# Position bias: two fp16 parts with a scale found on the chip in place of three bf16 parts, tables in blocks of 32 columns, one clamp on GpSimd

## The chip, the cores and the metric

One core of one Trainium2 chip. The metric is the device time of one execution, in microseconds; a profiled execution is read for the reasons. Engines in the rows: PE (TensorE matmuls), PEld (its weight loads), DVE (VectorE), ACT (ScalarE), POOL (GpSimd), SP (SyncE, which here only issues DMAs).

## The reference

Attention over 4 batches, 8 heads, 576 positions and 64 dimensions, all in fp32, with a bias on the scores that a small network makes from the positions, then a gated layer (2304 tokens, 512 wide, 1536 hidden):

```python
scores = scale * np.matmul(q, k.transpose(0, 1, 3, 2))
psi_rel = np.log1p(np.abs(rel)); psi_i = np.log1p(np.maximum(pos[:, None], 1.0))
x = (psi_rel / psi_i)[..., None]          # 576 x 576
h = np.maximum(x @ w1 + b1, 0.0)          # hidden 32
bias = h @ w2                             # 576 x 576 x 8 heads
attn = softmax(scores + bias); out = attn @ v
out = ((sigmoid(x @ w_gate) * (x @ w_val)) @ w_out)   # x: attention output, 2304 x 512
```

## The kernel before

Three stages follow each other: the position bias (to about 108 us of the span), attention (to about 370 us), the gated layer. Inside the stages the instructions of each engine stand in the order in which the program writes them; only matmuls, DMA landings and the other engines' progress set when each runs.

**The bias.** A hidden unit is active or not, depending on position; where it is active it adds `w1*w2*x + b1*w2`. So the bias of a query row i, column j and head h is `A*x + B`, where A and B are sums over the active units. The kernel makes the 0/1 switches first (tiles `ind` and `far`, 128 partitions = 4 columns times 32 units), and then adds up the coefficients by matmul: the switches are the stationary side (128 by 128), the coefficients `cfs` the moving side (64 columns: A and B, 8 heads, 4 groups). As a coefficient is fp32 and the matmul takes 16-bit input, `cf` (eight times the product of weights, line 311) is cut into three bf16 parts (lines 394 and 396), and `sums` (line 354) issues one matmul for each part with the same switches.

The stage runs over nine chunks of 64 columns (`c`, loop at 398). `switches(c)` gives a chunk's twelve `one` (two matmuls of 288 columns, line 332, and an eviction by ACT, line 337, or for four of chunk 0 by DVE, line 335) and three `apart` (comparisons on DVE, line 350); those of chunk c+1 are issued between the matmuls of chunk c at places listed in `YPOS` and `DPOS`. A chunk has five blocks of query rows, in the order `BORD` = 0, 1, 4, 2, 3. A block of 128 rows is 16 `sums`, block 4 (64 rows) is 8, so a chunk has 72 `sums`. After a block, `leave` (line 358) multiplies A by the table `xt` on DVE (line 364; 377 for block 4) and adds B (line 372): for blocks 1, 2, 3 on DVE straight from PSUM, in two instructions (heads 0 to 5, and 6 and 7), for block 0 (except in the last chunk) and block 4 after a copy by ACT (line 367) on POOL (lines 372, 382). The sums have two PSUM buffers of one block, the switches' matmuls two of their own.

**The order on the queues at the start.** SP issues small, lt(0), the tables xt, then lt(1). DVE runs `edges`, the weights `wy`, lines 303 to 305, and then what `own` holds: twelve switches in the order of `OWN` = 0 to 5 and 8 to 13; `CFI` says at which of them the five steps begin that cut `cf` (lines 394, 396), one at each switch. POOL makes `cf` (lines 308, 311) from the small load alone.

**Beside it,** `conv` (`narrow_ahead`, line 734) turns nine blocks of fp64 weights into fp32, one step after each block of rows: ACT takes the size (201), DVE clamps (204), shifts (207) and merges (210, 213), SP stores (750). `begun()` lets attention's first loads and preparation run in chunks 2, 6, 7 and 8.

**Attention** (line 542) reads the bias in the softmax's first instruction (line 567, 576 columns of one head and block of 128 rows); a unit is nine such steps, there are 16 units.

Of the kernel before, what the change touches and what calls it, by code (L numbers as in the profile page):

```python
# [39 lines left out]
CFI = 1  # L40
# [37 lines left out]
def host_layout(data):  # L78
# [12 lines left out]
        axis=1)), **data}  # L91
# [57 lines left out]
def tile_kernel(ctx, tc, q, k, v, small, w_gate, w_val, w_out, steps, lpos, xtab, lx, out, phases="0AB"):  # L149
# [8 lines left out]
    with ExitStack() as right, ExitStack() as att:  # L158
# [7 lines left out]
        biases = over.tile([128, 24, S], F32, name="bias0"), keep.tile([128, 8, S], F32, name="bias3")  # L166
# [11 lines left out]
        with tc.manual_schedule():  # L178
            bias(tc, small, steps, lpos, xtab, lx, biases, biasL, moe, lambda: next(attn))
        if "A" in phases:  # L180
            for _ in attn:
                pass
            att.close()
            if "B" in phases:
                moe.run()
        else:
            nc.sync.dma_start(out=out[0:512, 0:512].rearrange("(c p) j -> p c j", p=128), in_=biases[1][:, 4:8, 0:512])


def narrow(nc, t, lo, hi, eng, sized=None):  # L190
# [6 lines left out]
    def size():  # L197
        if sized:
            sized.tensor_scalar(out=t, in0=hi, scalar1=0x7FFFFFFF, scalar2=None, op0=ALU.bitwise_and)
        else:  # L200
            nc.scalar.activation(out=f, in_=hi.bitcast(F32), func=AF.Abs)
# [16 lines left out]
def bias(tc, small, steps, lpos, xtab, lx, biases, biasL, moe, begun):  # L218
# [6 lines left out]
    with ExitStack() as ph:  # L225
# [22 lines left out]
        lt = load_lx(0)  # L248
        dist = cp.tile([128, 2 * S], F16, name="dist")
# [10 lines left out]
        warm = ip.tile([128, 2, S], BF16, name="ind0")[:, 0, 0:512]  # L260
# [45 lines left out]
        cf = cp.tile([128, 2, H, 4], F32, name="cf")  # L306
        for ab in range(2):
# [3 lines left out]
            nc.gpsimd.tensor_scalar(out=cf[:, ab], in0=cf[:, ab], scalar1=wb[:, ab:ab + 1], scalar2=8.0, op0=ALU.mult, op1=ALU.mult)  # L311
        conv = moe.narrow_ahead(pool("cvw", 2), pool("cvm", 2))

        def switches(c, lt):

            np_, at = len(DPAIRS), S - 64 * c - 4 * DPAIRS[0]
            far = ip.tile([128, np_, 2 * S], BF16, name="far")
            pair = {i: far[:, n].rearrange("p (z s) -> p z s", z=2) for n, i in enumerate(DPAIRS)}
            pair.update({i: ip.tile([128, 2, S], BF16, name=f"ind{i}") for i in OWN if i < 8})
# [34 lines left out]
        def sums(o, st):  # L354
            for part in range(3):
                nc.tensor.matmul(out=o, lhsT=st, rhs=cfs[:, part], start=(part == 0), stop=(part == 2))  # L356

        def leave(ps, c, blk):
# [6 lines left out]
            if blk in BPOOL and c < NCH - 1 or blk == 4:  # L365
                rest, add = tp.tile([128, 2, H, 32], F32, name="brest")[:, 0:n], nc.gpsimd
                nc.scalar.activation(out=rest, in_=ps[:, 0:n, 1], func=AF.Copy)
            else:
                rest, add = ps[:, 0:n, 1], nc.vector
            if blk < 4:  # L370
                for t, h0, h1 in ((biases[0], 0, 6), (biases[1], 6, 8)):
                    add.tensor_tensor(  # L372
# [810 lines left out]
```

## Time and profile before

| | us |
|---|---|
| median of 3 runs (lowest, highest) | 803.34 (801.77, 805.56) |
| the profiled execution | 804.37 |
| its span | 802.60 |
| PE busy | 774.0 (96%) |
| DVE busy | 634.8 (79%) |
| ACT busy | 511.5 (64%) |
| POOL busy | 343.7 (43%) |

The span is what the profile covers, from the first to the last instruction; the execution's time has 1.8 us more around it. Busy time is the union of an engine's instructions, which overlap at their ends, so a mean length times a count is more than the busy time; a matmul's length holds its latency. Shares over the whole span say little about a stage, so the rows below are cut by stage.

### The profile page before, as it was taken

To read this page: it belongs to the slowest core of one execution; us is meant where nothing else is said; L and a number is where in the kernel's file an instruction comes from. 1 tells how busy PE (TensorE), PEld (TensorE's weight loads), DVE (VectorE), ACT (ScalarE), POOL (GpSimd) and SP (SyncE) were. 2 spreads that over 40 slices of the span, in tenths; PEclk is the share of its full clock that TensorE was granted. 3 is DMA by queue.
4 is the path that set the end of the run, shared out by engine and by line. 5 is a ranking of instruction groups with operands and counts; after the bars stand their busy time and mean duration, and the time that the engine had idled before them with its cause. 6 is when DMAs were issued, how large, how long until landed. Compare 5 with 4: busy or idle time off the path is not lost.

```text
span 802.6 us, 17329 instructions
## 1 busy us (share of the span) xinstructions
PE 774.0 (96%) x6356; PEld 722.8 (90%) x6356; DVE 634.8 (79%) x1301; ACT 511.5 (64%) x1094; POOL 343.7 (43%) x400
## 2 busy tenths in 40 slices
PE   7999989999999998899999999999999999999997
PEld 4888879999999998888998999889999999999996
DVE  6788888999999999896799899877877865656542
ACT  5888769989989987784444443554545546444442
POOL 1233559999989998951000000126233231523200
PEclk8999999999999999999999999999999999999999
DMA  5543434654664667747999633376334306321202
GB/s 198 152 147 126 130 97 125 176 167 131 180 172 127 180 178 205 212 125 234 367 313 297 203 132 131 118 220 220 111 106 145 105 27 212 129 73 64 75 1 79
DMA packets 66693, 124.21 MB, mean 155 GB/s; under 512 B 7344, under 2 KB 28976, under 8 KB 66608
## 3 DMA queue, kind: packets, MB, share of 16 engines
q1 hardware_dynamic: 64688, 120.15, 48.8%
q10 hardware_dynamic: 1920, 2.95, 1.2%
q8 instruction: 50, 0.82, 0.4%
q14 instruction: 35, 0.29, 0.1%
HBM read 86.04 MB, written 27.60 MB: 142 GB/s over the span
## 4 chain that ended last, share of the span: by engine, by line
PE 73%; DVE 13%; ACT 5%; DMA 4%; issue 3%; SPq 1%; POOL 0%; ACTq 0%; DVEq 0%
PE po L916 16%; PE pg L1018 12%; PE pu L1018 9%; PE sc L563 8%; PE acc L648 7%; PE pt L586 6%; PE pu L892 4%; PE pg L892 4%; PE bps L356 3%; DMA xin<-xs 2%; PE y L332 2%; DVE btmp L364 2%; ACT ind L337 1%; DVE en L567 1%; DVE bias L372 1%
## 5 line engine op out<-in xcount | busy, mean ns | idle before, releaser
L975 POOL TENSOR_TENSOR ws<-wm 128x256 f32<-128x256 f32 x44 | 41.4, 940 | 301.6 <-DMA wm<-scratch 147.0
L570 ACT ACTIVATE en<-en,mn 128x576 f32<-128x576 f32 x144 | 111.5, 774 | 31.7 <-DVE mn L567 30.7
L1018 PE MATMUL pg<-xq,wv 128*128 128x384 f32 x576 | 117.2, 338 | 1.0 <-ACT c L1044 1.0
L563 PE MATMUL sc<-k,QS 128*128 128x288 f32 x640 | 112.2, 301 | 1.4 <-DVE bias L372 0.6
L1018 PEld LDWEIGHTS pg<-xq,wv 128*128 128x128 f32 x576 | 103.2, 188 | 9.7 <-ACT c L1044 1.7
L567 DVE CUSTOM_DVE_ANT_0 en<-sc,bias 128x576 f32<-128x576 f32 x128 | 93.9, 751 | 7.4 <-PE sc L563 6.4
L1024 DVE TENSOR_TENSOR c<-pu,c 128x384 f32<-128x384 f32 x72 | 40.1, 557 | 74.5 <-PE pu L1018 29.3
L563 PEld LDWEIGHTS sc<-k,QS 128*128 128x128 f32 x640 | 92.0, 189 | 2.8 <-PE sc L563 0.8
L586 PE MATMUL pt<-ident,en 128*128 128x128 f32 x576 | 87.5, 275 | 3.1 <-DVE aL L486 1.9
L916 PE MATMUL po<-wo,gh 128*128 128x512 f32 x288 | 89.6, 392 | 0.0
L1018 PE MATMUL pu<-xq,wv 128*128 128x384 f32 x432 | 87.6, 337 | 0.4 <-DVE g L902 0.3
L1018 PEld LDWEIGHTS pu<-xq,wv 128*128 128x128 f32 x432 | 76.6, 188 | 3.3 <-DVE g L902 0.8
L648 PE MATMUL acc<-aH,vv 128*128 128x288 f32 x240 | 76.3, 334 | 3.2 <-DVE xe L651 3.0
L586 PEld LDWEIGHTS pt<-ident,en 128*128 128x128 f32 x576 | 68.7, 141 | 6.6 <-ACT en L570 3.4
L486 DVE TENSOR_TENSOR aL<-pt,aH 128x512 fp32r<-128x512 f32 (+1 forms) x112 | 66.6, 607 | 7.1 <-ACT aH L485 7.1
L356 PE MATMUL bps<-cfs,ind 128*128 128x64 bf16 x1458 | 67.4, 193 | 3.1 <-DVE bias L372 2.4
L337 ACT ACTIVATE ind<-y 128x576 bf16<-128x576 f32 x100 | 62.1, 653 | 10.5 <-PE y L332 8.2
L356 PEld LDWEIGHTS <-ind 128*128 128x128 bf16 x1458 | 58.6, 98 | 9.6 <-DVE bias L372 4.2
L648 PE MATMUL acc<-aL,vv 128*128 128x288 f32 x240 | 67.1, 296 | 0.0
L1036 ACT ACTIVATE gh<-c 128x384 fp32r<-128x384 f32 x48 | 25.2, 526 | 62.9 <-DVE c L1034 62.9
L490 POOL TENSOR_TENSOR aL<-ar,aH 128x512 fp32r<-128x512 f32 x48 | 62.4, 1300 | 4.0
L1044 ACT ACTIVATE c<-pg 128x384 f32<-128x384 f32 x72 | 35.1, 487 | 38.0 <-PE pg L1018 37.1
(152 smaller groups left out, 1913.4 us busy)
## 6 DMA issues: line engine op xcount, KB each, us to landing
wm<-scratch SPq DMA_DIRECT2D x48, 256.0 KB, 2.6
wo<-parts SPq DMA_DIRECT2D x24, 512.0 KB, 5.2
kr<-in_k_dram SPq DMA_DIRECT2D x32, 288.0 KB
QS<-part SPq DMA_DIRECT2D x64, 144.0 KB, 2.5
xs<-xe SPq DMA_DIRECT2D x32, 288.0 KB, 3.5
xin<-xs SPq DMA_DIRECT2D x48, 192.0 KB, 4.0
parts<-w SPq DMA_DIRECT2D x12, 512.0 KB, 10.0
vr<-in_v_dram SPq DMA_DIRECT2D x16, 320.0 KB, 3.6
```

The lines of the kernel that those rows point to most:

```text
L337: nc.scalar.activation(out=o, in_=y[:, :, 0:HF], func=AF.Sigmoid, scale=float(2.0 ** 64))
L356: nc.tensor.matmul(out=o, lhsT=st, rhs=cfs[:, part], start=(part == 0), stop=(part == 2))
L486: return lambda: nc.vector.tensor_tensor(out=lo, in0=ps, in1=hi.bitcast(F32), op=ALU.subtract)
L490: nc.gpsimd.tensor_tensor(out=lo, in0=src, in1=hi.bitcast(F32), op=ALU.subtract)
L563: nc.tensor.matmul(out=ps[:, e, 0:HF], lhsT=l, rhs=r[:, HF * e:HF * e + HF], start=(i == 0), stop=(i == len(mms) - 1))
L567: nc.vector.tensor_tensor_reduce(out=half(en), in0=ps[:, :, 0:HF], in1=half(nbias), scale=-0.125, scalar=3.0e38, op0=ALU.add, op1=ALU.min, ...
L570: nc.scalar.activation(out=en, in_=en, func=AF.Exp, bias=mn, scale=-1.0, accum_out=sm)
L586: nc.tensor.transpose(pt[:, J], en[:, 128 * J:128 * J + 128], ident)
L648: nc.tensor.matmul(out=acc[:, 0:HF], lhsT=l, rhs=r, start=(i == 0), stop=(i == len(mms) - 1))
L892: self.nc.tensor.matmul(out=(pg, pu)[z], lhsT=l, rhs=r, start=(kc == 0 and i == 0), stop=(kc == 3 and i == 2))
L916: self.nc.tensor.matmul(out=po, lhsT=l[:, tt], rhs=r, start=(first and i == 0), stop=(last and i == 2))
L1018: nc.tensor.matmul(out=p, lhsT=W[i][:, l, at + kc], rhs=V[b][:, r, kc], start=(new and n == 0), stop=(n == 5), skip_group_check=not new)
```

## The change

Coefficients: `cf` is scaled by `up`, a power of two, and cut into two fp16 parts; the switches are fp16 tiles. The scale comes from the largest absolute product of weights, found on the chip: a new input `wide` (w2 repeated over 128 partitions, 128 KB) is loaded by SP after lt(0), POOL multiplies it with w1 and b1 (2 x 8 x 32 values and a floor of 2^-100), DVE reduces to the largest and takes its exponent bits, POOL scales `up` and the inverse `un`. The tables xt are multiplied by `un` on POOL, and B is multiplied by `un` where it is evicted: as the scale of ACT's copy, or by a scalar_tensor_tensor in place of DVE's tensor_tensor. `CFI` goes from 1 to 8, so the now three steps stand at the ninth to eleventh switch. The bias tables become blocks of 32 columns, [18, 4, heads, 32], written block by block and read by the softmax through a pattern of 32-column runs. `narrow_ahead` passes GpSimd as the engine of the clamp.

```diff
@@ -37,7 +37,7 @@
 WARM = 12
-CFI = 1
+CFI = 8
@@ -88,7 +88,7 @@
         [np.repeat(w1, 128, 0), np.repeat(b1, 128, 0), picks(), np.tile(w1.T, (4, 1)), np.tile(b1.T, (4, 1)), np.tile(w2, (4, 1))],
-        axis=1)), **data}
+        axis=1)), "wide": np.repeat(w2.T.reshape(1, H * HID), 128, 0), **data}
@@ -163,7 +163,7 @@
         make_identity(nc, ident)
-        biases = over.tile([128, 24, S], F32, name="bias0"), keep.tile([128, 8, S], F32, name="bias3")
+        biases = over.tile([128, 18, 4, 6, 32], F32, name="bias0"), keep.tile([128, 18, 4, 2, 32], F32, name="bias3")
@@ -246,6 +243,8 @@
         lt = load_lx(0)
+        wd = cp.tile([128, H, HID], F32, name="wide")
+        nc.sync.dma_start(out=wd.rearrange("p h m -> p (h m)"), in_=wide)
@@ -257,7 +256,7 @@
             nc.sync.dma_start(out=xt[64 * e:64 * e + 64, 4, 0:S - 32 * e], in_=xtab[512:576, 32 * e:S])
-        warm = ip.tile([128, 2, S], BF16, name="ind0")[:, 0, 0:512]
+        warm = ip.tile([128, 2, S], F16, name="ind0")[:, 0, 0:512]
@@ -304,19 +303,35 @@
         cf = cp.tile([128, 2, H, 4], F32, name="cf")
+        fit = cp.tile([128, 3], F32, name="fit")
+        big, up, un = (fit[:, i:i + 1] for i in range(3))
+        both = cp.tile([128, 2 * H * HID + 1], F32, name="both")
+        nc.gpsimd.memset(both[:, 2 * H * HID:], 2.0 ** -100)
+        nc.gpsimd.tensor_tensor(
+            out=both[:, 0:2 * H * HID].rearrange("p (z h m) -> p z h m", z=2, h=H),
+            in0=wd.rearrange("p (o h) m -> p o h m", o=1).to_broadcast([128, 2, H, HID]),
+            in1=wr.rearrange("p z (o m) -> p z o m", o=1).to_broadcast([128, 2, H, HID]), op=ALU.mult)
+        nc.vector.tensor_reduce(out=big, in_=both, axis=mybir.AxisListType.X, op=ALU.max, apply_absolute_value=True)
+        nc.vector.tensor_scalar(out=up.bitcast(I32), in0=big.bitcast(I32), scalar1=0x7F800000, scalar2=0x7F800000, op0=ALU.bitwise_and, op1=ALU.bitwise_xor)
+        nc.vector.tensor_scalar(out=un.bitcast(I32), in0=big.bitcast(I32), scalar1=0x7F800000, scalar2=None, op0=ALU.bitwise_and)
+        for o, z in ((up, 13), (un, -11)):
+            nc.gpsimd.tensor_scalar(out=o, in0=o, scalar1=float(2.0 ** z), scalar2=None, op0=ALU.mult)
...
                 in1=group.rearrange("p (o g) -> p o g", o=1).to_broadcast([128, H, 4]), op=ALU.mult)
-            nc.gpsimd.tensor_scalar(out=cf[:, ab], in0=cf[:, ab], scalar1=wb[:, ab:ab + 1], scalar2=8.0, op0=ALU.mult, op1=ALU.mult)
+            nc.gpsimd.tensor_scalar(out=cf[:, ab], in0=cf[:, ab], scalar1=wb[:, ab:ab + 1], scalar2=up, op0=ALU.mult, op1=ALU.mult)
+        for blk in BORD:
+            x = xt[:, blk, 0:S if blk < 4 else S - 32]
+            nc.gpsimd.tensor_scalar(out=x, in0=x, scalar1=un, scalar2=None, op0=ALU.mult)
...
             np_, at = len(DPAIRS), S - 64 * c - 4 * DPAIRS[0]
-            far = ip.tile([128, np_, 2 * S], BF16, name="far")
+            far = ip.tile([128, np_, 2 * S], F16, name="far")
             pair = {i: far[:, n].rearrange("p (z s) -> p z s", z=2) for n, i in enumerate(DPAIRS)}
-            pair.update({i: ip.tile([128, 2, S], BF16, name=f"ind{i}") for i in OWN if i < 8})
+            pair.update({i: ip.tile([128, 2, S], F16, name=f"ind{i}") for i in OWN if i < 8})
@@ -352,8 +367,8 @@
         def sums(o, st):
-            for part in range(3):
-                nc.tensor.matmul(out=o, lhsT=st, rhs=cfs[:, part], start=(part == 0), stop=(part == 2))
+            for part in range(2):
+                nc.tensor.matmul(out=o, lhsT=st, rhs=cfs[:, part], start=(part == 0), stop=(part == 1))
@@ -364,14 +379,17 @@
                 rest, add = tp.tile([128, 2, H, 32], F32, name="brest")[:, 0:n], nc.gpsimd
-                nc.scalar.activation(out=rest, in_=ps[:, 0:n, 1], func=AF.Copy)
+                nc.scalar.activation(out=rest, in_=ps[:, 0:n, 1], func=AF.Copy, scale=un)
...
                 for t, h0, h1 in ((biases[0], 0, 6), (biases[1], 6, 8)):
-                    add.tensor_tensor(
-                        out=t[:, blk::4, js].rearrange("p h (s j) -> p s h j", s=2),
-                        in0=rest[:, :, h0:h1], in1=tmp[:, :, h0:h1], op=ALU.add)
+                    o, a, b = t[:, 2 * c:2 * c + 2, blk], rest[:, :, h0:h1], tmp[:, :, h0:h1]
+                    if add is nc.gpsimd:
+                        add.tensor_tensor(out=o, in0=a, in1=b, op=ALU.add)
+                    else:
+                        o, a, b = (z.rearrange("p s h j -> p s (h j)") for z in (o, a, b))
+                        add.scalar_tensor_tensor(out=o, in0=a, scalar=un, in1=b, op0=ALU.mult, op1=ALU.add)
@@ -383,16 +401,16 @@
         ind, own, far = switches(0, lt)
-        cfs = cp.tile([128, 3, 2, H, 4], BF16, name="cfs")
+        cfs = cp.tile([128, 2, 2, H, 4], F16, name="cfs")
...
             part, sub = divmod(i - CFI, 2)
-            if part in range(3):
+            if part in range(2):
...
                     nc.vector.tensor_copy(out=cfs[:, part], in_=cf)
-                elif part < 2:
+                elif part < 1:
@@ -551,12 +569,12 @@
             h, it = divmod(s, 4)
-            nbias = biases[0][:, 8 * p + s] if p < 3 else biases[1][:, s]
+            nbias = biases[0][:, :, it, 2 * p + h] if p < 3 else biases[1][:, :, it, h]
...
         else:
-            nbias = biasL[:, p]
+            nbias = biasL[:, p].rearrange("p (j m) -> p j m", m=32)
@@ -565,7 +583,8 @@
             nc.vector.tensor_tensor_reduce(
-                out=half(en), in0=ps[:, :, 0:HF], in1=half(nbias), scale=-0.125, scalar=3.0e38,
+                out=en.rearrange("p (e j m) -> p e j m", e=2, m=32), in0=ps[:, :, 0:HF].rearrange("p e (j m) -> p e j m", m=32),
+                in1=nbias.rearrange("p (e j) m -> p e j m", e=2), scale=-0.125, scalar=3.0e38,
@@ -746,7 +765,7 @@
                 going.append([
-                    lambda: None, lambda: None, *narrow(nc, m, w[:, :, :, 0], w[:, :, :, 1], nc.vector),
+                    lambda: None, lambda: None, *narrow(nc, m, w[:, :, :, 0], w[:, :, :, 1], nc.gpsimd),
...
```

## Rows read from the trace of the kernel before

**Rows 1.** Windows: length; busy of PE, PEld, DVE, ACT, POOL; clock; DMA share; GB/s

```profile
16.67:27.79 11.12, 10.23 (x250) 9.27 (x247) 7.36 (x15) 9.49 (x16) 3.21 (x6) 1.00 0.36 114
27.79:90.05 62.26, 59.12 (x1459) 53.26 (x1456) 53.28 (x115) 53.49 (x94) 23.27 (x40) 1.00 0.48 149
90.05:100.27 10.22, 9.32 (x243) 8.32 (x239) 8.85 (x20) 7.16 (x13) 6.48 (x10) 1.00 0.47 137
100.27:108.35 8.08, 5.62 (x159) 5.06 (x155) 7.21 (x17) 1.67 (x2) 3.14 (x5) 1.00 0.40 118
124.20:139.40 15.20, 15.20 (x124) 14.99 (x123) 13.86 (x37) 13.79 (x34) 14.28 (x16) 1.00 0.56 146
```

**Rows 2.** Timeline of PE, chunk 0: start us, length us, instruction, count

```profile
15.07 0.69 PE L356 MATMUL bps<-cfs,ind 128*128 128x64 bf16 x18 [0.31 <-ACT ind L337]
...
15.77 0.69 PE L356 MATMUL bps<-cfs,ind 128*128 128x64 bf16 x18
```

**Rows 3.** Groups by line and shape, 27.79 to 90.05: busy us, mean ns, idle

```profile
L356 PE MATMUL bps<-cfs,ind 128*128 128x64 bf16 x990 | 46.7, 193 | 0.6 <-DVE bias L372 0.2 <-ACT brest L367 0.2
...
L356 PE MATMUL bps<-cfs,far 128*128 128x64 bf16 x324 | 18.3, 193 | 0.0
L364 DVE TENSOR_TENSOR btmp<-bps,xt 128x512 f32<-128x512 f32 x25 | 17.2, 689 | 4.5 <-PE bps L356 4.2
```

**Rows 4.** Timeline of ACT, chunk 3

```profile
53.05 1.79 ACT L337 ACTIVATE ind<-y 128x576 bf16<-128x576 f32 x3
```

**Rows 5.** Timeline of DVE, chunks 3 and 4; brackets: idle before, releaser

```profile
54.63 0.69 DVE L364 TENSOR_TENSOR btmp<-bps,xt 128x512 f32<-128x512 f32 x1 [0.92 <-PE bps L356]
...
56.03 0.42 DVE L204 TENSOR_SCALAR cvm<-cvm 128x512 f32<-128x512 f32 x1
...
57.99 0.42 DVE L207 TENSOR_SCALAR cvm<-cvm 128x512 int32<-128x512 int32 x1
```

**Rows 6.** Timeline of DVE, the start

```profile
6.89 0.35 DVE L295 SCALAR_TENSOR_TENSOR btmp<-wh,small,btmp 128x128 f32<-128x128 bf16 x1
7.16 0.29 DVE L297 TENSOR_TENSOR btmp<-btmp,wh 128x128 f32<-128x128 f32 x1
...
10.15 0.19 DVE L394 CAST cfs<-cf 128x64 bf16<-128x64 f32 x1
...
14.79 0.76 DVE L335 TENSOR_SCALAR ind<-bps 128x576 bf16<-128x576 f32 x1
```

**Rows 7.** Timeline of POOL, the start

```profile
3.94 0.25 POOL L308 TENSOR_TENSOR cf<-small 128x32 f32<-128x32 f32 x1 [2.18 <-DMA small<-in_small_dram]
...
5.04 0.52 POOL L311 TENSOR_SCALAR cf<-cf,small 128x32 f32<-128x32 f32 x1
```

**Rows 8.** Groups by line and shape, 0 to 200 us

```profile
L479 POOL TENSOR_SCALAR aH<-ar 128x512 fp32r<-128x512 f32 x18 | 11.1, 619 | 4.2 <-PE sc L563 2.1 <-ACT ar L599 1.9
...
L499 ACT ACTIVATE part<-qr 128x576 fp32r<-128x576 f32 x8 | 5.5, 684 | 0.0
...
L281 ACT ACTIVATE pos<-pos,et 128x576 f32<-128x576 f32 x1 | 0.8, 774 | 1.7 <-DVE et L278 1.7
```

**Rows 9.** Timeline of POOL, chunks 7 and 8

```profile
99.40 0.66 POOL L479 TENSOR_SCALAR k<-kr 128x576 fp32r<-128x576 f32 x1
```

**Rows 10.** Timeline of DVE, chunks 7 and 8

```profile
99.56 0.78 DVE L207 TENSOR_SCALAR cvm<-cvm 128x512 int32<-128x512 int32 x1
...
105.39 0.69 DVE L364 TENSOR_TENSOR btmp<-bps,xt 128x512 f32<-128x512 f32 x1 [0.73 <-PE bps L356]
```

**Rows 11.** The page's costliest groups of instructions, whole span

```profile
L567 DVE CUSTOM_DVE_ANT_0 en<-sc,bias 128x576 f32<-128x576 f32 x128 | 93.9, 751 | 7.4 <-PE sc L563 6.4
...
L563 PEld LDWEIGHTS sc<-k,QS 128*128 128x128 f32 x640 | 92.0, 189 | 2.8 <-PE sc L563 0.8
...
L356 PEld LDWEIGHTS <-ind 128*128 128x128 bf16 x1458 | 58.6, 98 | 9.6 <-DVE bias L372 4.2
...
L490 POOL TENSOR_TENSOR aL<-ar,aH 128x512 fp32r<-128x512 f32 x48 | 62.4, 1300 | 4.0
```

More of the change, by code (lines that the diff above doesn't have):

```diff
@@ L148, in tile_kernel @@
 @with_exitstack
-def tile_kernel(ctx, tc, q, k, v, small, w_gate, w_val, w_out, steps, lpos, xtab, lx, out, phases="0AB"):
+def tile_kernel(ctx, tc, q, k, v, small, wide, w_gate, w_val, w_out, steps, lpos, xtab, lx, out, phases="0AB"):
     nc = tc.nc
@@ L178, in tile_kernel @@
         with tc.manual_schedule():
-            bias(tc, small, steps, lpos, xtab, lx, biases, biasL, moe, lambda: next(attn))
+            bias(tc, small, wide, steps, lpos, xtab, lx, biases, biasL, moe, lambda: next(attn))
         if "A" in phases:
@@ L186, in tile_kernel, with narrow @@
         else:
-            nc.sync.dma_start(out=out[0:512, 0:512].rearrange("(c p) j -> p c j", p=128), in_=biases[1][:, 4:8, 0:512])
-def narrow(nc, t, lo, hi, eng, sized=None):
+            nc.sync.dma_start(out=out[0:512, 0:512].rearrange("(c p) j -> p c j", p=128), in_=biases[1][:, 0:16].rearrange("p a b h j -> p a (b h j)").rearrange("p (c z) m -> p c (z m)", c=4)[:, :, 0:512])
+def narrow(nc, t, lo, hi, eng):
     f = t.bitcast(F32)
     def size():
[L198 to L201, printed above, removed]
+        nc.scalar.activation(out=f, in_=hi.bitcast(F32), func=AF.Abs)
     def clamp():
@@ L215, in narrow, with bias @@
     return size, clamp, low, top, tail
-def bias(tc, small, steps, lpos, xtab, lx, biases, biasL, moe, begun):
+def bias(tc, small, wide, steps, lpos, xtab, lx, biases, biasL, moe, begun):
     nc = tc.nc
```

## The prediction

> **What bounds the kernel now.** I read the table of windows first, cut where the first table multiply of a chunk starts (line 364). The position bias is built in nine chunks before attention. In the six whole chunks from 27.79 to 90.05 us PE is busy 59.12 of 62.26 us, ACT 53.49, DVE 53.28 and POOL 23.27 [rows 1]. So a chunk takes 62.26/6 = 10.38 us, in which PE works 9.85 (95%), ACT 8.92, DVE 8.88: PE is the bound, but two other engines stand 0.9 us below it. After this stage PE is busy 15.20 of 15.20 us in a unit of attention [rows 1], so what the stage gives back moves the rest forward as a block, and the change touches nothing behind it but the layout that the softmax reads.
>
> The timeline gives PE's price: 18+6 small matmuls take from 15.07 to 15.77, 0.70/24 = 29.2 ns each, although a row calls one 193 ns long (they are pipelined) [rows 2, 3]. A chunk has 72 products with three matmuls, 216 x 29.2 = 6.31 us of PE; the rest of its 9.85, 3.54 us, are mostly the 24 wide matmuls of line 332. (The 990+324 rows in six chunks are 219 a chunk, the cut being in the middle of a block [rows 3].) DVE's timeline shows the same bound: at 54.63 it had been idle 0.92 us for PE [rows 5]. ACT's evictions of line 337 go back to back at about 0.60 us (three in 1.79) [rows 4].
>
> **The change, part by part.** **Two parts for three.** 72 matmuls fewer a chunk: 72 x 29.2 = 2.10 us, PE's work falls to 7.75. No row shows a matmul in fp16. The nearest are these bf16 ones, same shape, same bytes: 29.2 ns. The other end is the fp32 kind, whose weight loads are named 189 ns against 98 here [rows 11], about twice, so 58 ns. I take the nearer row. The Trainium skill, "TensorE: Matmul & The Clock Gate", section "Weight-path perf modes", says the fast weight load is on for 128 weights of any type that isn't FP32; by it fp16 costs what bf16 does, and no run here shows it yet. The 0/1 tables are now written as fp16, two bytes as before: nothing.
>
> **What is late next.** PE at 7.75 no longer holds the chunk; ACT (8.92) and DVE (8.88) do, and their own changes decide.
>
> ACT: its two evictions a chunk at line 367 get a scale read per partition. The nearest rows: an Exp with such a scale over 576 elements 774 ns, a plain Copy of the same shape 684 [rows 8]; so 0 to 0.09 us each, 0 to 0.18 a chunk. I take half: ACT 9.0.
>
> DVE: the clamp (line 204, 0.42 us [rows 5]) goes to POOL, nine of them in some seven chunks: -0.5 us a chunk. Against that six adds of a chunk (line 372) become scalar_tensor_tensor with a per-partition scalar. Such an instruction over 128 elements took 0.35 us, a plain tensor_tensor of that size right behind it 0.29 [rows 6]: +0.06 each, +0.36 a chunk, or 0 if the length alone counts. DVE 8.4 to 8.75. The output in runs of 32 columns costs nothing I can see: line 364 already reads in runs of 32 and takes 689 ns for 512 elements, the softmax without them 751 for 576, 1.35 and 1.30 ns an element with the fixed part in it [rows 3, 11].
>
> POOL has room (23.27 of 62.26 busy [rows 1]) for nine clamps of about 0.62 us (its copy of 512 elements: 619 ns [rows 8]). But the clamp now queues behind POOL's adds of the same block, and DVE's next conversion step (line 207) waits for it, with DVE's next table work queued behind. Where the block is 0 or 4, POOL starts those adds late, so two or three of the nine can cost DVE 0.3 to 0.6 us, hidden in part. I take 0.3 us in all. A row speaks against the change: line 207 took 0.78 us instead of 0.42 at 99.56 while POOL ran a copy from 99.40 to 100.06 [rows 5, 9, 10]: the two engines get in each other's way. The Trainium skill, "SBUF - State Buffer", section "Who interferes with whom", has the rule: one port pair is shared, locked for a whole instruction, and the other engine stands still; the row agrees (0.36 us lost). By it a clamp of 0.62 us on POOL could take from DVE more than the 0.42 it gives; that is the first rival.
>
> So ACT at 9.0 is the longest, DVE close behind. PE now fills 95% of a chunk as the bound; with two near-equal engines I take the same share, 9.0/0.95 = 9.45 us. Ends: 8.92 (ACT alone, no stall) and 10.0 (first rival).
>
> **The start.** The new 128 KB load goes into SP's queue ahead of the table loads and delays them by little; nobody waits for those before 16.7. POOL then makes 512 products (1.30 us as its other 128x512 [rows 11]), early, if the load is there. On DVE the reduction stands where the first cast of line 394 stood (10.15 [rows 6]): about 0.69 as line 364 [rows 3], two one-column operations of 0.1, so the queue is 0.9 later at 11.1. POOL then scales twice and makes the coefficients, four operations that took from 3.94 to 5.56 before [rows 7]; with the two scalings about 2.3 us, done near 13.4. DVE reaches the first cast (CFI 8) only around 14.1, and saves two of the five small operations of 0.2. The last cast is at about 15.3, the last switch (14.79 before [rows 6]) starts at about 15.3 too, and PE starts its products near 15.4 instead of 15.07, with a third fewer of them ahead of the first add. Net 0.2 us late; ends: 0.3 early, and 3 late if the load only lands when the first loads are all through. POOL's scaling of the tables (5 x 0.67 us [rows 9]) comes just behind, the first block done before it is used.
>
> **The last chunk** has DVE busy 7.21 of 8.08 us [rows 1]; its idle is one wait of 0.73 for PE [rows 10], of which PE gives back most, while eight scalar adds cost 0.5. Zero, within 0.6 either way.
>
> **The sum.** Chunks 1 to 7 (62.26 + 10.22 us [rows 1]): 7 x (10.35 - 9.45) = 6.3. Chunk 0, 11.12 us with ACT at 9.49 [rows 1], goes to 9.49/0.95 = 10.0: 1.1. Less 0.2 for the start and 0.3 for the clamps: 6.9 us. The profiled execution took 804.37 us (span 802.60), so 797.5. The median of the runs is 1.0 below it, so 796.4 from there; I forecast 796.8. Perfect overlap gives 7 x (10.35 - 8.92) + 11.12 - 9.49 = 11.6, from the median 791.7. Chunks of 10.0 us give 7 x 0.35 = 2.5, with 0.6 of chunk 0, less 0.3 and a start 0.9 late: 1.9, or 802.5 from the profiled time and 801.4 from the median; a start 3 us late takes all of that.
>
> **The rivals.** **DVE takes the place of PE.** The scalar costs 0.36 a chunk, and clamps and adds collide on the shared way into memory: 0.62 x 1.25 clamps = 0.78 a chunk. DVE then needs 8.75 + 0.78 = 9.5, /0.95 = 10.0 us: gain 2 to 3 us, about 801.5. For it: the 0.78 us row. Against: POOL is idle six tenths of the stage, line 207 met POOL in one row and took 0.42 elsewhere. Chance 0.20.
>
> **Slower: the softmax pays for the blocks.** Line 567 now reads its table in 18 pieces of 32 columns, far apart, and writes in the same shape. A unit of attention has nine of them and DVE is busy 13.86 of 15.20 us [rows 1]: 1.34 spare, 149 ns each. If each grew by x, PE would lose (9x - 1.34) us in each of 16 units; the 6.9 us of gain are gone at x = 0.198, a softmax of 0.95 us against 0.75 now. At 1.0 us: 0.9 x 16 = 14.4, less 6.9: about 811. Against it: line 364's price per element above. Chance 0.05.
>
> **Slower: fp16 runs slower on PE.** With p ns a matmul PE needs 144p + 3.54; at p = 44 it is back at 9.85 us and the start is lost; at 58 ns a chunk is 11.9/0.95 = 12.5, eight chunks give 17 us, about 821. Nothing in the trace speaks for it. Chance 0.03. That the change doesn't do what it says can be read directly: 144 matmuls a chunk.
>
> PE's clock is no rival: the granted clock is 1.00 in all of these windows (the 2.4 GHz level), also in the last chunk with PE busy 5.62 of 8.08 [rows 1], a lower share than I expect in any chunk but the last.
>
> **How the numbers follow.** Forecast (pitch 8.9 to 9.8) 0.72, DVE bound 0.20, slower 0.08. The range 791.5 to 802.0 takes in the first two. Half a per cent, 4 us, is about what a measurement of this kernel can tell from no change: below 799.3 counts as faster, 0.72; the DVE case is the same, 0.20; slower 0.08.
>
> **What would show it.** In the trace after: bps matmuls at about 29 ns, 1296 in all; chunks of 9.2 to 9.7 us with PE near 80%, ACT and DVE above 90%, the waits now PE's for ACT (line 337) and DVE (line 372); line 372 at 0.06 us more or nothing; clamps of 0.62 on POOL; first add of a table within 1 us of 16.67; softmax at 0.75. I am wrong if chunks stay at 10 us with DVE full, if PE's first product slips past 17 us, or if attention's units leave 15.2 us.

## The result, and the profile after

The median went from 803.43 us (801.77 to 805.56, 4 runs) to 809.66 us (809.01 to 810.12, 4 runs): ratio 1.008, 95% interval 1.0056 to 1.0104. The kernel is 6.4 us slower (the ratio times 803.4); the forecast was 6.5 us faster. The profiled execution took 809.34 us, its span is 807.6, 5.0 more than before.

The windows of after, cut as in [rows 1] (columns as there), and one microsecond of its last chunk:

```profile
17.39:28.38 10.99, 9.12 (x184) 7.81 (x181) 8.74 (x16) 9.37 (x17) 8.66 (x10) 1.00 0.36 129
28.38:94.22 65.84, 49.77 (x1011) 41.33 (x1008) 53.50 (x106) 54.14 (x94) 37.58 (x48) 1.00 0.44 137
94.22:103.92 9.70, 7.42 (x169) 6.21 (x166) 8.82 (x18) 6.84 (x12) 7.72 (x9) 1.00 0.40 120
103.92:111.89 7.97, 4.48 (x103) 4.15 (x98) 7.27 (x14) 1.76 (x2) 6.31 (x8) 0.79 0.38 109
108.00:109.00 1.00, 0.85 (x17) 0.86 (x18) 1.00 (x2) 0.11 (x1) 0.59 (x1) 0.50 0.00 0
```

PE has less to do, as promised: 49.77 us in six chunks in place of 59.12 (8.30 a chunk; the prediction had 7.75). Yet the six chunks take 65.84 us in place of 62.26: 10.97 each. No engine is full: DVE 81%, ACT 82%. POOL went from 23.27 to 37.58 us. The 5.0 us of span are 0.72 at the start (first add at 17.39, not 16.67), 2.93 in chunks 0 to 7 (86.53 against 83.60), 1.15 from there to the first matmul of the scores (7.97 against 6.82; in before that matmul starts at 107.09, inside the last window of the stage), and 0.2 in all the rest.

The groups by line and shape of after, 0 to 112 us, that hold the change (us busy, mean ns, idle before):

```profile
L201 POOL TENSOR_SCALAR cvm<-cvm 128x512 f32<-128x512 f32 x9 | 17.9, 1992 | 0.5
L392 DVE SCALAR_TENSOR_TENSOR bias<-bps,fit,btmp 128x384 f32<-128x384 f32 x27 | 16.7, 618 | 1.0
...
L392 DVE SCALAR_TENSOR_TENSOR bias<-bps,fit,btmp 128x128 f32<-128x128 f32 x27 | 9.2, 341 | 0.0
...
L326 POOL TENSOR_SCALAR xt<-xt,fit 128x576 f32<-128x576 f32 x4 | 6.9, 1733 | 0.0
```

In before, 0 to 200 us:

```profile
L372 DVE TENSOR_TENSOR bias<-bps,btmp 128x384 f32<-128x384 f32 x28 | 15.6, 558 | 1.0
...
L372 DVE TENSOR_TENSOR bias<-bps,btmp 128x128 f32<-128x128 f32 x28 | 7.9, 281 | 0.0
...
L210 DVE SCALAR_TENSOR_TENSOR cvm<-cvw,cvm 128x512 int32<-128x512 int32 x9 | 6.1, 682 | 0.0
```

And from the page's costliest groups, over the whole span:

```profile
L585 DVE CUSTOM_DVE_ANT_1 en<-sc,bias 128x576 f32<-128x576 f32 x128 | 93.8, 752 | 7.3 <-PE sc L581 6.3
...
L371 PE MATMUL bps<-cfs,ind 128*128 128x64 f16 x972 | 52.8, 195 | 17.7 <-DVE bias L392 10.9
```

The clamp on POOL (line 201) takes 1.99 us, not 0.62; the scaling of a table (line 326) 1.73, not 0.67. The adds with a scalar take 618 and 341 ns; without it they took 558 and 281 in before. The softmax (line 585) is where it was [rows 11], and the products (line 371) wait 10.9 us for DVE.

The list of waits of after, 17 to 113 us (us in all, times, longest):

```profile
ACT brest L382 <- DVE btmp L379: 10.9, 8, 2.9
PE bps L371 <- DVE bias L392: 10.9, 18, 1.9
...
DVE cvm L204 <- POOL cvm L201: 6.2, 4, 2.2
```

DVE stands still 6.2 us for the clamp, with the table work of the next block queued behind that wait; and PE stands still behind DVE's adds.

Last chunk of after, timelines of DVE, POOL and PE:

```profile
105.43 1.14 DVE L207 SCALAR_TENSOR_TENSOR cvm<-cvw,cvm 128x512 int32<-128x512 int32 x1
106.50 0.68 DVE L379 TENSOR_TENSOR btmp<-bps,xt 128x512 f32<-128x512 f32 x1
...
108.00 1.14 DVE L210 SCALAR_TENSOR_TENSOR cvm<-cvw,cvm 128x512 int32<-128x512 int32 x1
```

```profile
104.62 1.41 POOL L508 TENSOR_TENSOR k<-kr,k 128x576 fp32r<-128x576 f32 x1
106.00 1.11 POOL L497 TENSOR_SCALAR k<-kr 128x576 fp32r<-128x576 f32 x1
107.19 1.40 POOL L508 TENSOR_TENSOR k<-kr,k 128x576 fp32r<-128x576 f32 x1
109.55 1.98 POOL L400 TENSOR_TENSOR biasL<-brest,btmp 64x128 f32<-64x128 f32 x4 [0.96 <-DVE btmp L395]
```

```profile
103.90 0.51 PE L371 MATMUL bps<-cfs,ind 128*128 128x64 f16 x12
104.25 0.28 PE L371 MATMUL bps<-cfs,far 128*128 128x64 f16 x4
...
108.14 0.82 PE L371 MATMUL bps<-cfs,ind 128*128 128x64 f16 x12 [1.93 <-DVE bias L392]
108.78 0.40 PE L371 MATMUL bps<-cfs,far 128*128 128x64 f16 x4
...
111.89 0.77 PE L581 MATMUL sc<-k,QS 128*128 128x288 f32 x4 [0.52 <-POOL biasL L400]
```

The same adds of POOL in the last chunk of before:

```profile
104.74 1.97 POOL L382 TENSOR_TENSOR biasL<-brest,btmp 64x128 f32<-64x128 f32 x4 [3.12 <-DVE btmp L377]
```

Twelve fp16 matmuls take 104.25 - 103.90 = 0.35 us, 29 ns each, the price of bf16 [rows 2]. After a wait of 1.93 us for DVE the same twelve take 0.64, 53 ns each: the granted clock is 0.50 there (the lower level). The two merges (lines 207, 210; 210 and 213 in before), 0.68 us in before, take 1.14 where POOL's line 508 runs.

The merges, not the clock, explain the 1.15 us. The scores' first matmul waits for POOL's adds of block 4 (line 400), and these for DVE. From the chunk's first multiply to these adds before took 4.47 us (104.74 - 100.27), after takes 5.63 (109.55 - 103.92). The 1.16 us more are two merges that go on for 0.46 us longer each and two pairs of adds with a scalar, 0.12 each. The products at the lower clock, from 108.14 on, are of the blocks behind block 4. In e1 below, with the clamp off POOL, both merges of this chunk take 0.68 us again.

### The profile page after: what moved, and what is told of

It is laid out like the page before. It is cut to its first block, busy times and chain, and to the rows that moved or that the text cites. A ratio compares the mean times of both kernels' runs of the same rounds, so it can differ in the third digit from the quotient of the medians.

```text
span 807.6 us, 16048 instructions
## 1 busy us (share of the span) xinstructions
PE 760.4 (94%) x5708; PEld 706.7 (88%) x5708; DVE 639.6 (79%) x1293; ACT 512.8 (64%) x1094; POOL 374.7 (46%) x418
## 4 chain that ended last, share of the span: by engine, by line
PE 68%; DVE 8%; DMA 3%; ACT 2%; issue 2%; POOL 1%; SPq 1%; ACTq 0%; DVEq 0%
PE po L935 16%; PE pg L1037 12%; PE pu L1037 9%; PE sc L581 8%; PE acc L667 7%; PE pt L605 6%; PE pg L911 4%; PE pu L911 4%; PE pt L625 1%; DVE en L585 1%; DMA xin<-xs 1%; DVE w L876 1%; ACT en L589 1%; DMA ww<-in_moe_w_out_dram 1%; DVE aL L504 1%
## 5 line engine op out<-in xcount | busy, mean ns | idle before, releaser
L371 PE MATMUL bps<-cfs,ind 128*128 128x64 f16 x972 | 52.8, 195 | 17.7 <-DVE bias L392 10.9
L371 PEld LDWEIGHTS <-ind 128*128 128x128 f16 x972 | 45.6, 99 | 26.5 <-issue 11.6
L352 ACT ACTIVATE ind<-y 128x576 f16<-128x576 f32 x100 | 60.6, 652 | 8.8 <-PE y L347 8.2
```

What stands on the lines that cost most here:

```text
L352: nc.scalar.activation(out=o, in_=y[:, :, 0:HF], func=AF.Sigmoid, scale=float(2.0 ** 64))
```

## The experiments

Theory A: the clamp on POOL costs more than the two parts bring. Rival B: the adds with a scalar and the search for the scale do. A third question came with the first results: why two parts alone bring so little.

**e1: the clamp back on DVE.**

```diff
-                    lambda: None, lambda: None, *narrow(nc, m, w[:, :, :, 0], w[:, :, :, 1], nc.gpsimd),
+                    lambda: None, lambda: None, *narrow(nc, m, w[:, :, :, 0], w[:, :, :, 1], nc.vector),
```

> The changed kernel with one edit: the clamp of the nine weight blocks back on DVE. In the changed kernel the clamp on POOL has a mean of 1.99 us (0.42 on DVE before) and DVE waited 6.2 us for it. Theory A (the clamp on POOL is the loss: 6.2 us of waits, the rest by delayed queues): 798 to 802 us, chunks of 9.3 to 9.8 us. Rival B (the per-partition scalar on DVE's adds, 0.06 us on 56 instructions, and on ACT's copies, 0.09 us on 17, make DVE and ACT the bound): 806 to 809 us, chunks near 10.5. Rival C (the start: POOL's scaling of the tables takes 8.5 us and holds its later adds): 806 to 809 us, the first chunk still 11 us and the rest as in B.

It took 805.62 us, a ratio to before of 1.0026 (95% interval 1.0016 to 1.0036, as in all that follow), between the times that A and B had forecast. The six chunks:

```profile
28.24:90.84 62.60, 50.09 (x1027) 41.43 (x1023) 55.21 (x114) 54.03 (x94) 23.21 (x40) 1.00 0.48 146
```

10.43 us a chunk in place of 10.97, although DVE has more to do. So the clamp on POOL costs 4.0 us; but without it the change still brings nothing and is 2 us slower than before.

**e2: before, with only the clamp on POOL** (the diff of e1 the other way round).

> The kernel before with one edit: the clamp on POOL. Theory A: the clamp takes 2.0 us here too, and DVE, which has 1.4 us idle in a chunk of 10.4, hides only part of the waits: 806 to 809 us. Rivals B and C: within 1.5 us of the kernel before, 802 to 805.

It took 807.84 us, 1.0052 (1.0040 to 1.0064). The move alone costs over 4 us also where PE has its three parts. Its six chunks:

```profile
26.51:91.91 65.40, 60.08 (x1458) 53.64 (x1455) 51.38 (x107) 54.11 (x94) 37.63 (x48) 1.00 0.46 141
```

Here too DVE stands still for the clamp, 5.6 us in three waits.

**e3: after, with a plain multiplication on POOL in the clamp's place**.

```diff
+        if eng is nc.gpsimd:
+            eng.tensor_scalar(out=f, in0=f, scalar1=1.0, scalar2=1.0, op0=ALU.mult, op1=ALU.mult)
+            return
         eng.tensor_scalar(out=f, in0=f, scalar1=float(2.0 ** -15), ...
```

> The changed kernel with POOL's clamp replaced by a copy of the same tile in the same place (multiply by 1.0 twice, the form that takes 0.62 us for 128x512 in attention); the clamp itself is left out. It asks what makes the clamp 2.0 us long. If the operation does (max and min are slow on POOL): 0.62 to 0.7 us a copy and, by theory A, 799 to 803 us. If the place does (collisions with DVE, unaligned tiles): it stays near 2.0 us and the time near 809. Rival B: short copies but still 806 to 809 us.

It took 806.09 us, 1.0035 (1.0022 to 1.0048). The instruction takes 701 ns in the mean:

```profile
L202 POOL TENSOR_SCALAR cvm<-cvm 128x512 f32<-128x512 f32 x9 | 6.3, 701 | 0.4
```

With the length that the prediction assumed, the move costs 0.5 us against e1 (the prediction had 0.3). So it is the clamp's 1.99 us that costs, not its place in POOL's queue.

**e4: before, with two fp16 parts alone**, the scale a constant 8 as before.

```diff
-            for part in range(3):
-                nc.tensor.matmul(out=o, lhsT=st, rhs=cfs[:, part], start=(part == 0), stop=(part == 2))
+            for part in range(2):
+                nc.tensor.matmul(out=o, lhsT=st, rhs=cfs[:, part], start=(part == 0), stop=(part == 1))
...
-        cfs = cp.tile([128, 3, 2, H, 4], BF16, name="cfs")
+        cfs = cp.tile([128, 2, 2, H, 4], F16, name="cfs")
```

> The kernel before with the matmul part of the change alone: two fp16 parts instead of three bf16 parts, with the constant scale of 8 that was there; no search for a scale, no scaling back, tables and clamp as before. It prices what fewer matmuls are worth by themselves. By the step of the forecast (PE 7.75 us a chunk, ACT 8.9 and DVE 8.9 the new bound at 95%): chunks of 9.4 us, 794 to 797 us. If coupling between DVE, ACT and PE eats it: chunks of 9.9 or more, 800 to 803 us.

It took 800.15 us, 0.9963 (0.9951 to 0.9976): a gain of 3.0 us, where the prediction's sum had 7.4 for chunks of 9.45 and 10.0 us.

```profile
25.21:86.51 61.30, 51.04 (x1025) 42.44 (x1021) 53.33 (x114) 53.13 (x94) 23.24 (x40) 0.97 0.50 150
```

PE has 8 us less, the chunks are 10.2 us, and DVE fills 87% of them. (The clock of 0.97 is one stretch at 0.50, the lower level, from 69 to 72 us, after PE had been busy 0.44 of 2 us from 66 to 68; e12 and e13 below, without one, have 10.03 us.)

**e6: e4 without three of the five conversion steps on DVE** (shift and merges left out).

```diff
-                    lambda: None, lambda: None, *narrow(nc, m, w[:, :, :, 0], w[:, :, :, 1], nc.vector),
+                    lambda: None, lambda: None, *narrow(nc, m, w[:, :, :, 0], w[:, :, :, 1], nc.vector)[:2], *[lambda: None] * 3,
```

> e4 with DVE's three later steps of the nine weight conversions left out (0.42 + 0.68 + 0.68 us each, 16 us of DVE in the stage; those weights are then wrong). Rival E: DVE sets the pace, chunks fall to 9.0 to 9.3 us, 790 to 794 us. Theory D: the chain in block 0 and ACT's order stay, 797 to 799.5 us.

**e12: e4 with two of ACT's twelve evictions a chunk fewer** (two switches are zeros from chunk 1 on).

```diff
+            if c:
+                pair[5] = still
...
-            return pair, [lambda i=i: one(i) for i in OWN], ...
+            return pair, [lambda i=i: one(i) for i in OWN if c == 0 or i not in (5, 13)], ...
```

> The counterpart of e6: e4 with two of twelve switch evictions (and their matmuls) left out from chunk 1 on, a tile of zeros in their place (the bias is then wrong): 1.2 us of ACT and 0.5 us of PE less a chunk, 9.6 us of ACT in all. If DVE alone sets the pace: 799 to 801 us. If ACT does so as much as DVE (e6 gave 7.2 us for 16 us of DVE): 795 to 797 us.

e6 takes 792.97 us, 0.9872 (0.9859 to 0.9886); e12 801.47, 0.9973 (0.9961 to 0.9985). Their six chunks, e6 first:

```profile
25.50:81.39 55.89, 48.70 (x1018) 41.43 (x1015) 43.42 (x94) 52.53 (x94) 21.12 (x40) 1.00 0.57 172
```

```profile
25.83:86.01 60.18, 47.01 (x1006) 39.19 (x1003) 53.16 (x114) 46.14 (x83) 23.23 (x40) 1.00 0.48 148
```

10 us off DVE in these chunks bring 5.4 there against e4, 4.3 against the 60.18 of e12 and e13; in the medians e6 is 7.2 us below e4. 7 us off ACT bring nothing. With two parts DVE sets the pace. Only in e6 is ACT much the fullest engine, at 94% of 9.32 us: near the chunk that the prediction had (9.45), with 10 us of DVE's work gone.

**e8: e1 without the scalars.**

```diff
-                nc.scalar.activation(out=rest, in_=ps[:, 0:n, 1], func=AF.Copy, scale=un)
+                nc.scalar.activation(out=rest, in_=ps[:, 0:n, 1], func=AF.Copy)
...
-                        add.scalar_tensor_tensor(out=o, in0=a, scalar=un, in1=b, op0=ALU.mult, op1=ALU.add)
+                    add.tensor_tensor(out=o, in0=a, in1=b, op=ALU.add)
```

> e1 (the changed kernel with the clamp on DVE) with the scaling back of B left out: plain tensor_tensor adds on DVE for the scalar_tensor_tensor, and ACT's copy without a scale; the bias is then off in B by a factor. These cost 56 x 0.06 on DVE and 17 x 0.09 on ACT, 4.9 us of busy time. Theory F (they carry most of the 5.5 us between e1 and e4): 801 to 803 us. Rival G (the start carries it): 804.5 to 806 us.

It took 802.03 us, 0.9991 (0.9980 to 1.0003): 3.6 us less than e1.

```profile
28.02:88.27 60.25, 49.78 (x1024) 41.40 (x1021) 53.25 (x115) 52.90 (x94) 23.32 (x40) 1.00 0.52 151
```

DVE has 1.96 us less than in e1, ACT 1.13, and the six chunks are 2.35 shorter. The two were not taken out one by one; as 7 us off ACT brought nothing in e12, the loss is put down to DVE, and what the scalars add there goes into the time in full.

**e9: e1 with constant scales** (8 and 1; no wide load, no products, no reduction, no scaling of the tables).

```diff
+        nc.gpsimd.memset(up, 8.0)
+        nc.gpsimd.memset(un, 1.0)
...
-        for blk in BORD:
-            x = xt[:, blk, 0:S if blk < 4 else S - 32]
-            nc.gpsimd.tensor_scalar(out=x, in0=x, scalar1=un, scalar2=None, op0=ALU.mult)
```

> e1 with the search for the scale left out: constants in its place (8 and 1), no load of the repeated weights, no products, no reduction, no scaling of the tables on POOL; the adds keep their scalar. Theory F: 803 to 805 us, the first add of a table 0.6 us earlier than in e1 at the same clock at the start. Rival G: 800 to 801.5 us.

It took 804.40 us, 1.0013 (1.0004 to 1.0022): the search costs 1.2 us.

**e13: e9 without the scalars, `CFI` 1**, so only the two parts and the 32-column blocks are left of the change.

```diff
-CFI = 8
+CFI = 1
...
-                        add.scalar_tensor_tensor(out=o, in0=a, scalar=un, in1=b, op0=ALU.mult, op1=ALU.add)
+                    add.tensor_tensor(out=o, in0=a, in1=b, op=ALU.add)
```

> e1 with both parts of e8 and e9 taken out, and the first cast back at the second switch (CFI 1): what is left against e4 is the layout of the tables in blocks of 32 columns, on the writing side and in the softmax. If the layout costs nothing: e4's time, 799.5 to 801 us, softmax at 0.75 us. If it costs what e8 and e9 leave unexplained (0.7 us): near 801.

It took 799.94 us, 0.9957 (0.9942 to 0.9971), e4's time: the blocks cost nothing. The medians of before beside these runs lie between 803.1 and 803.6, so the kernels form a ladder from before to after: before 803.3, two parts 800.15 (e4), blocks 799.94 (e13), scalars and the later casts 804.40 (e9), search 805.62 (e1), clamp 809.66 (after). In steps -3.2, -0.2, +4.5, +1.2 and +4.0 us, each to about 1 us by the intervals. A and B are both right: by these steps either alone eats the gain. For B e1 shows it; for A it is a sum, as two parts with the clamp on POOL and nothing else were not run.

**e5: e4, with ACT's copy of block 0 issued ahead of DVE's multiply.** In e4 ACT's copy waits for the multiply of the same block, and with it the evictions queued behind it.

```diff
-            if blk < 4:
-                x = xt[:, blk, js].rearrange("p (s o j) -> p s o j", s=2, o=1)
-                nc.vector.tensor_tensor(out=tmp, in0=ps[:, :, 0], in1=x.to_broadcast([128, 2, H, 32]), op=ALU.mult)
-            if blk in BPOOL and c < NCH - 1 or blk == 4:
+            pooled = blk in BPOOL and c < NCH - 1 or blk == 4
+            if pooled:
                 rest, add = tp.tile([128, 2, H, 32], F32, name="brest")[:, 0:n], nc.gpsimd
                 nc.scalar.activation(out=rest, in_=ps[:, 0:n, 1], func=AF.Copy)
...
+            if blk < 4:
+                x = xt[:, blk, js].rearrange("p (s o j) -> p s o j", s=2, o=1)
+                nc.vector.tensor_tensor(out=tmp, in0=ps[:, :, 0], in1=x.to_broadcast([128, 2, H, 32]), op=ALU.mult)
```

> e4 with one order turned round in block 0: ACT's copy out of PSUM is issued ahead of DVE's multiplication (as block 4 has it), so ACT no longer waits for DVE, but DVE for ACT. In e4 ACT stood idle 6.2 us for that multiplication in all and PE 4.8 us for that copy. Theory D (what keeps a chunk near 10 us once PE has slack is this chain of waits PE - DVE - ACT - PE in block 0): 796 to 799 us. Rival E (DVE and ACT are simply full): 799.5 to 801 us, DVE's wait for ACT taking the place of ACT's for DVE.

The median is 810.13 us (lowest 804.51, highest 813.96), 1.0069 (1.0041 to 1.0097): slower, against both expectations, and by an uncertain amount. The trace is of its fastest run, 804.51 us, 4.4 above e4; what made most of the others longer still is not shown. Timelines of e5, then e4, at the same place:

```profile
46.00 1.90 POOL L373 TENSOR_TENSOR bias<-brest,btmp 128x384 f32<-128x384 f32 x2 [4.17 <-DVE btmp L370]
...
46.10 1.49 DVE L350 TENSOR_TENSOR far<-dist,edge 128x1024 f16<-128x1024 f16 x1
```

```profile
46.15 0.60 ACT L367 ACTIVATE brest<-bps 128x512 f32<-128x512 f32 x1 [1.09 <-DVE btmp L364]
46.28 0.69 DVE L350 TENSOR_TENSOR far<-dist,edge 128x1024 f16<-128x1024 f16 x1
...
46.89 1.41 POOL L372 TENSOR_TENSOR bias<-brest,btmp 128x384 f32<-128x384 f32 x2 [4.33 <-ACT brest L367]
```

ACT's wait goes, but POOL's add now starts with DVE's comparison of two tiles, which takes 1.49 us in place of 0.69 (mean of the 18 comparisons: 952 ns against 685, 4.8 us in all). In e4 the late copy happened to hold POOL back until the comparison was nearly through. The Trainium skill, "SBUF — State Buffer", section "Who interferes with whom", says that a DVE instruction with two inputs in SBUF contends with a GpSimd instruction that reads there, and that one with at most one SBUF input does not, outside the modes that use two ports. The traces agree: here 0.69 to 1.49, the merges above 0.68 to 1.14, while line 379, whose other input is in PSUM, keeps 0.68 beside POOL's line 497. Not every step with one SBUF input is spared: line 207 of before took 0.78 in place of 0.42 beside POOL [rows 9, 10]. Which mode it ran in no trace shows.

**e11: e4, with the copy and POOL's adds of block 0 issued in the middle of block 1. e15: the same on before, with three parts.**

```diff
+            if blk in BPOOL and c < NCH - 1:
+                def rest_later():
+                    rest = tp.tile([128, 2, H, 32], F32, name="brest")[:, 0:n]
+                    nc.scalar.activation(out=rest, in_=ps[:, 0:n, 1], func=AF.Copy)
+                    for t, h0, h1 in ((biases[0], 0, 6), (biases[1], 6, 8)):
+                        nc.gpsimd.tensor_tensor(...)
+                return rest_later
...
+                    if later and n == 1 and i == 8:
+                        later()
+                        later = None
```

> e4 with ACT's copy of block 0 and POOL's two adds issued later, in the middle of block 1, behind two more evictions of switches, so that ACT has work while DVE multiplies. ACT's 6.2 us of waits for DVE in e4 should go to under 2. If that wait is worth something: 797 to 799 us. If DVE alone sets the pace (e6): 799.5 to 801, with the same chunks of 9.9 us.

> The kernel before, three bf16 parts and all, with only e11's order: the copy of block 0 and POOL's adds issued in the middle of block 1. If the order is worth something only when PE has slack: 802.5 to 804 us, as before. If it is worth 3.4 us by itself: 799 to 801 us.

e11 took 796.77 us, 0.9916 (0.9902 to 0.9930), by chance the forecast's time, and better than both kernels; e15 took 801.19, 0.9981 (0.9972 to 0.9990), between its two expectations. The six chunks of e11, and three of the waits of e4 and one of e11, 17 to 113 us:

```profile
25.87:83.78 57.91, 47.81 (x1025) 40.56 (x1021) 53.44 (x114) 53.77 (x94) 23.47 (x40) 1.00 0.52 158
```

```profile
DVE btmp L364 <- PE bps L356: 7.5, 10, 1.7
...
ACT brest L367 <- DVE btmp L364: 6.2, 7, 1.2
PE bps L356 <- DVE bias L372: 5.5, 13, 1.4
```

```profile
ACT brest L368 <- DVE btmp L364: 0.6, 2, 0.4
```

9.65 us a chunk, DVE and ACT at 92 and 93%, with e4's work. ACT's wait for the multiply falls from 6.2 us in e4 to 0.6, and PE's for ACT's evictions of the switches (line 337) from 5.3 to 1.1. So part of the missing gain sat in the order of ACT's queue: 3.4 us with two parts, 2.0 with three (1.5 by the ratio).

**e10: eight forms of POOL's instruction in the clamp's place**, one for each conversion, 128 x 512 values in place; one run, for the lengths alone.

```diff
+        n = FORMS.pop(0) if eng is nc.gpsimd else 0
...
+        elif n == 2:
+            eng.tensor_scalar(out=f, in0=f, scalar1=1.0, scalar2=None, op0=ALU.mult)
+        elif n == 3:
+            eng.tensor_scalar(out=f, in0=f, scalar1=float(2.0 ** -15), scalar2=None, op0=ALU.max)
...
```

> The changed kernel, with another form of tensor_scalar on POOL for each of the nine clamps, all on the same 128x512 fp32 tile in place: in order 1 multiply by 1.0 twice, 2 multiply by 1.0 once, 3 max with a constant, 4 multiply by a per-partition scalar, 5 that and a multiply by 1.0, 6 add 0 and multiply by 1.0, 7 max and multiply by 1.0, 8 a copy, 9 the clamp (max and min); eight of the nine weight blocks are left without their clamp. Only the lengths count here. e3 gave 0.70 us for form 1, the changed kernel 1.99 for form 9 and 1.73 for a table scaled by a per-partition scalar (576 elements). If max and min are what is slow: 3, 7 and 9 at 1.5 us or more, the others at 0.6 to 0.8. If every form but the double multiply is slow: 2 to 8 all above 1.3 us. The time lies between e3's 806 and 809.5 us.

Timeline of POOL, in order: mult and mult; mult alone; max alone; mult by a scalar per partition; the same and mult; add and mult; max and mult; copy:

```profile
31.38 0.65 POOL L208 TENSOR_SCALAR cvm<-cvm 128x512 f32<-128x512 f32 x1
...
42.16 1.50 POOL L210 TENSOR_SCALAR cvm<-cvm 128x512 f32<-128x512 f32 x1
...
47.19 1.81 POOL L212 TENSOR_SCALAR cvm<-cvm 128x512 f32<-128x512 f32 x1
...
56.87 1.57 POOL L214 TENSOR_SCALAR cvm<-cvm,one 128x512 f32<-128x512 f32 x1
...
66.94 0.69 POOL L216 TENSOR_SCALAR cvm<-cvm,one 128x512 f32<-128x512 f32 x1
...
73.86 0.61 POOL L218 TENSOR_SCALAR cvm<-cvm 128x512 f32<-128x512 f32 x1
...
84.58 1.93 POOL L220 TENSOR_SCALAR cvm<-cvm 128x512 f32<-128x512 f32 x1
...
90.01 0.96 POOL L222 COPY cvm<-cvm 128x512 f32<-128x512 f32 x1
```

The clamp follows at 99.98 with 1.92 us. Neither expected answer holds alone: the forms with a maximum are slow, and so is a single multiplication. Pairs of mult and add take about a third of a clamp's time. Why was not tried. Each form was timed once, and the place counts too. In e3 the same pair stands at all nine places: it takes 0.61 to 0.65 us at seven of them, but more at the third and the eighth, where DVE's merge (line 213, at 46.09 and 88.50) runs beside it:

```profile
46.24 1.01 POOL L202 TENSOR_SCALAR cvm<-cvm 128x512 f32<-128x512 f32 x1
...
88.70 0.96 POOL L202 TENSOR_SCALAR cvm<-cvm 128x512 f32<-128x512 f32 x1
```

So the copy's 0.96 us, at the eighth place, says nothing about its form, and some 0.4 us of the lone maximum's 1.81, at the third, may be the place.

**e14: all of the change's work, mended**: e1 with the order of e11, and POOL's scalings as pairs.

```diff
-            nc.gpsimd.tensor_scalar(out=x, in0=x, scalar1=un, scalar2=None, op0=ALU.mult)
+            nc.gpsimd.tensor_scalar(out=x, in0=x, scalar1=un, scalar2=1.0, op0=ALU.mult, op1=ALU.mult)
```

> The changed kernel with what the runs found mended, all its work kept: the clamp on DVE, the copy of block 0 issued in the middle of block 1 as in e11, and POOL's scalings of the tables and of the scale in the two-operation form (a second multiply by 1.0; 0.69 us in e10 against 1.57). If the prices add up: e11's 796.8, plus 3.6 for the scalars (e8), plus 0.5 to 1.2 for the search at the start (e9): 800.9 to 801.8 us, chunks of 9.9 to 10.0 us. If the scalars' price is hidden again by the looser order: 797.5 to 799.5. If the late copy helps only without the scalars: 804 or more.

It took 802.25 us, 0.9986 (0.9975 to 0.9997), slightly above what adding up the gains gave: with all of the change's work, mended, the kernel is about 1 us faster than before. The scaling of a table falls from 1733 to 739 ns:

```profile
L326 POOL TENSOR_SCALAR xt<-xt,fit 128x576 f32<-128x576 f32 x4 | 2.9, 739 | 0.0
```

## Why the prediction was wrong

**Right.** fp16 on PE costs 29 ns a matmul, with 972 + 324 = 1296 of them. The Trainium skill, "TensorE: Matmul & The Clock Gate", section "Weight-path perf modes", has the fast weight load on for 128 weights of a type other than FP32; the trace agrees. The scalar costs +60 ns an add, as taken from [rows 6], the softmax stays at 752 ns, and the rest of the program moves as a block. ACT's scale costs 0.09 us (687 against 598 ns), the upper end.

**Right in part by luck: the start,** 0.72 us late, within the microsecond that was allowed. That is one pair of profiles. In e2, which starts as before does, the first add is at 15.38, and after comes 2.0 us behind that:

```profile
15.38 0.69 DVE L364 TENSOR_TENSOR btmp<-bps,xt 128x512 f32<-128x512 f32 x1 [0.74 <-PE bps L356]
```

From 8 to 14 us the granted clock is 0.50 in before (the lower level), after PE had stood idle for 3.24 us, and 1.00 in e2, after 1.70 us; the small load also landed 0.39 us later in before. Kernels with the search have the first add between 17.15 and 17.57, e1 and e8 with less time at the lower clock than after.

**Wrong, first: the step "with two near-equal engines I take the same share", 9.0/0.95 = 9.45 us** (worked out, 9.47). The 95% was PE's share while PE was the one bound of before. Without PE's excess DVE, ACT and PE are a ring: ACT's copy waits for DVE's multiply, PE for a bank that ACT and DVE must empty, DVE for PE. In e13 a chunk takes 60.18/6 = 10.03 us, with 8.82 us of ACT and 8.88 of DVE (89%):

```profile
25.26:85.44 60.18, 49.80 (x1025) 41.45 (x1021) 53.27 (x115) 52.91 (x94) 23.23 (x40) 1.00 0.50 154
```

The gain of two parts is 3.0 to 3.4 us (e4, e13), not 6.3 + 1.1. e11 shows that the share is a matter of the order: 92% once one wait of the ring is taken out. e6 and e12 show which engine: DVE, not ACT, although ACT's busy time in before was 0.04 us a chunk the longer. The forecast's range began at the perfect overlap of ACT and did not reach the other side of before.

**Wrong, second: the scalars counted as free.** +0.36 us a chunk on DVE was rightly worked out (measured 1.96/6 = 0.33) and then dropped from the path because ACT was taken as the longest. They cost 3.6 us (e8).

**Wrong, third: the clamp's 0.62 us.** It was taken from the nearest row by shape, a copy that is not a maximum [rows 8]. It is 1.99. DVE gave up nine clamps of 0.43 us, 3.9 in all, but waited 6.2 us for POOL and lost more in its steps beside POOL: in the six chunks of after, with eight clamps less, DVE is only 1.71 us lighter than in those of e1. The step was priced at 0.3 us and cost 4.0; e3, with an instruction of 0.70 us, cost 0.5, so the mechanism was right and its size was not. A bound from both sides would have had [rows 11], line 490 at 1.30 us, as its far end, still short of 1.99.

**Wrong, without much effect: the scaling of the tables,** 5 x 0.67 taken, 8.49 us measured, from 14.37 to 22.86. POOL's adds of chunk 0 start only then. With the rest of the search it costs 1.2 us (e9). At the start, too, POOL met DVE: beside the products (line 310, 6.41 to 7.72 us) DVE's line 294 took 1.23 us, in before 0.35 [rows 6], and beside the first scaling the first cast (line 412) 0.72, in before 0.19.

**The rivals.** "DVE takes the place of PE" named the right mechanism: DVE as the bound, the scalar's 0.36, POOL and DVE in each other's way. But it used the same 95% and the clamp's 0.62 us, so it came out 2 to 3 us faster. With 1.99 us and 89% its sum is the slower case, but too slow: 8.75 + 1.25 x 1.99 = 11.24, over 0.89, is 12.6 us a chunk where 10.97 was measured, as DVE waited for only four of the nine clamps. The two slower rivals, softmax and fp16, did not occur. "PE's clock is no rival" held for the chunks; in the last one the clock fell to 0.50 behind the wait of 1.93 us, but the 1.15 us there went by DVE and POOL, as shown above.

## What to carry to other kernels

When the one full engine is relieved, the next chunk is not the next engine's busy time at the old fill: look at who waits for whom among the rest, and take an engine's share from a stage in which it already shares the bound. Until the bound is settled, count work added to any engine that is within a tenth of it in full: here that was so for DVE (e8), while work taken off ACT brought nothing (e12). An operation moved to another engine is priced from a row of the same operation there; where there is none, even the slowest row of that engine may be too short (1.30 us here, against 1.99).

## What was not expected of the hardware

- POOL's length of a tensor_scalar on 128 x 512 fp32 hangs on the form, at one size: 0.61 to 0.69 us for pairs of mult and add, 1.50 and 1.57 for one mult alone, 1.92 to 1.99 for the clamp, which DVE does in 0.43. Its place beside DVE's work adds 0.3 to 0.4 us at some places.
- Adding a second multiplication by 1.0 to POOL's single one makes it shorter: 1733 to 739 ns on 128 x 576.
- Taking away a wait lengthened a kernel: in e5, where POOL's add starts earlier, a DVE comparison beside it took 1.49 us in place of 0.69, and PE's waits for line 373 rose to 18.1 us, where e4's for line 372 were 5.5. That the first led to the second is argued from the trace; no run separated them.
